# Column weights turned by VectorE and sread in eight array tiles, a fourth batch in seven products, and a new order, in a cross-attention and star-ReLU kernel

## The chip, the cores and the metric

The kernel runs on one core of a Trainium2 chip. The metric is device time in microseconds (us), the median of several runs. The engines are TensorE (PE; PEld is its weight load), VectorE (DVE), ScalarE (ACT), GpSimd (POOL) and SyncE (SP). Transfers are started from the queues of POOL (loads of x and of the weights), SP (first load of x, all stores) and ACT (small loads).

## The reference

```python
# x (8, 8, 512, 64), state (8, 8, 32, 64): batch, head, rows, D
scores = x @ state.T / 8;  a  = softmax(scores, over the 32 states);  xread = a @ state
scores2 = state @ x.T / 8; a2 = softmax(scores2, over the 512 rows);  sread = a2 @ x
t = concat([xread, sread], rows)           # per batch 544 tokens of 8 heads x 64 = 512
h = t @ w_in                               # (4352, 512) @ (512, 2048)
out = (s * relu(h)**2 + b) @ w_out         # (4352, 2048) @ (2048, 512)
```

All eight batches need both softmaxes of the same score matrix: over the states (for xread) and over the rows (for sread).

## The kernel before

The work of each batch `b` is cut into pieces. A list of words, `ORDER` (L15 to L75), names them in the order in which they are issued, and L713 calls them one after another, so that each engine's own order follows from the list. A word is a piece's name with its arguments: `M.5.3.0` is piece `M` for batch 5, weight block 3. A last letter A, V or G puts the piece on ACT, DVE or POOL. Eight heads are kept as two groups `g` of four; a group's four heads lie in the four quarters of the 128 partitions.

Scores and the first softmax. `x` (L177) loads a batch, cast to f16, from POOL's queue; for batches above 2 a tiny POOL copy (L180) first waits until the batch before it has been turned. Batch 0 comes as f32 over SP's queue (L211 to L216) and is cast by `castx`. `xT` (L283) turns it with DVE in 32x32 blocks of f32 pairs. `T` (L291) makes the scores: 16 products on 32x32 tiles of the array, all 512 rows moving. `keep` (L306) copies scores for later use. `U`, `mu`, `D`, `E1`, `z`, `At`, `A` are the softmax over the states on DVE and ACT, in turned form, with `A` the turned-back weights; `D` and `At` can stand on POOL.

Layer one of the x tokens. `M` (L423) multiplies the state with a block of `w_in` (tiles of 64 rows by 32 columns) and `Mc` (L437) copies the result from PSUM; `l` (L469, half-width `lh`) multiplies `A` by it, two products of 512 columns, followed by a relu on ACT (L456). `s` (`sh`) squares blocks of it. `L` (L492) is layer two in its plain form: four products of 512 columns per word, 16 words per batch, and `out` (L512) evicts and stores.

The second softmax. `nm`, `nms`, `E2`, `a2` form the weights over the rows. `aps` (L391) turns them with eight TensorE transposes per batch into PSUM, `a2T` (L397) copies them out, `xn` (L188) loads x again with its rows on partitions, and `V` (L400) makes sread: per batch 32 products with 128 rows and 64 columns of weights and 32 moving columns, in one of the two-bank PSUM buffers. A word may name two batches (`V.5.2`). `srd` (L420) copies the result into `srdT`. `lsr`, `ssr`, `S_sr`, `P_sr`, `ev_sr` are the two layers for the sread tokens of all batches together, at the end.

Seven products. For batches 5, 6 and 7, and for sread, layer two is done as a 2x2 block product in seven half-size products instead of eight: `wsum` (L522) forms sums of weight blocks, `S` (L555) sums of activation blocks (in two halves each), `P` (L575) is half a product, eight matmuls of 256 columns (14 words per batch), `ev` (L589) evicts a block into a running sum, seven per batch, and `put` (L597) stores.

PSUM: `two_banks` (L130) gives one of two buffers of two banks each, one for `own` pieces and one for the others; `T`, `M`, `aps`, `V` and a few others share them. Layer one has two banks, layer two and the seven products two.

Of the kernel before, what the change touches and what calls it, by code (L numbers as in the profile page):

```python
# [15 lines left out]
    "win.0 win.1 wout.0 x.1 win.2 wout.1 win.3 wout.2 wout.3 idle.11 castx.1.0.V castx.0.0.A xT.0.0.0 "  # L16
    "casts.A turn.0.4.A pair.0.4 xT.0.1.0 T.0.1.0 U.0.0 mu.0.0 sb castx.1.1.A castx.0.1.A D.0.V.0 "
    "xT.0.0.1 idle.6 xT.0.1.1 E1.0.0 T.0.0.1 keep.0.0 M.0.0.1 Mc.0.0.A z.0.0 At.0.V.0 A.0.0 idle.4 "
    "M.0.1.1 Mc.0.1.A lh.0.0.0 U.0.1 mu.0.1 D.0.V.1 lh.0.2.0 keep.0.1 sh.0.0.0.V sh.0.2.0.V E1.0.1 z.0.1 "
    "At.0.V.1 L.0.1.0 lh.0.6.0 sh.0.6.0.G L.0.0.0 M.1.0.1 Mc.1.0.A lh.0.4.0 A.0.1 lh.0.6.1 xT.1.0 "  # L20
    "sh.0.4.0.G xT.1.1 T.1.1 U.1 lh.0.0.1 lh.0.4.1 lh.0.2.1 sh.0.2.1.G mu.1 M.0.2.0 Mc.0.2.A L.0.0.1 x.2 "
    "L.0.1.1 st D.1.V sh.0.6.1.V keep.1 l.0.9 l.0.8 M.0.3.1 Mc.0.3.V l.0.10 s.0.8.2.V cps.0 cps.1 E1.1 "
    "l.0.13 z.1 l.0.11 s.0.10.2.V At.1.V M.1.1.1 l.0.12 Mc.1.1.A l.0.14 l.0.15 L.0.0.2 s.0.12.2.A M.1.2.1 "
    "A.1 s.0.14.2.V Mc.1.2.A cps.2 cps.3 c L.0.1.2 l.1.1",
    "l.1.0 sh.0.0.1.V xT.2 M.1.3.1 x.3 L.0.0.3 bias out.0.0 l.1.2 Mc.1.3.V l.1.3 L.0.1.3 out.0.1 L.0.2.0 "
    "pair.4.16 sh.0.4.1.G turn.4.12.A L.0.2.1 l.1.4 turn.12.16.V T.2.1 keep.2 s.1.0.4.V l.1.5 l.1.6 "
    "L.0.2.2 l.1.8 U.2 mu.2 l.1.7 L.0.2.3 out.0.2 D.2.V l.1.9 s.1.8.2.V l.1.15 M.2.1.0 E1.2 z.2 M.2.0.1 "
# [12 lines left out]
    "M.4.2.1 wsum.T4.0.V s.3.8.4.V M.4.1.0 L.2.3.0 L.2.2.3 out.2.2 l.3.13 l.3.15 L.2.3.1 l.3.14 xT.5 "  # L40
    "Mc.4.2.V s.3.14.2.V Mc.4.1.A s.3.12.2.V wsum.T4.1.V",
    "l.4.0 L.2.3.2 L.2.3.3 out.2.3 T.5.1 V.4 srd.4 nm.5 U.5 l.4.1 nms.5.A x.6 L.3.0.0 E2.5.0 L.3.0.1 nm.2 "
    "l.4.2 mu.5 E2.5.1 L.3.1.0 D.5.V l.4.3 s.4.0.4.V L.3.1.1 L.3.0.2 l.4.4 xn.5 l.4.5 E1.5 z.5 L.3.0.3 "
    "nms.2.A M.4.3.0 out.3.0 M.5.0.1 Mc.4.3.A L.3.1.2 l.4.7 xn.2 Mc.5.0.A a2.5 l.4.6 s.4.4.4.V At.5.V "
    "E2.2.1 L.3.1.3 l.4.8 E2.2.0 L.3.2.0 out.3.1 aps.5 a2.2 a2T.5.A xT.6 L.3.2.1 L.3.2.2 l.4.9 L.3.2.3 "
    "l.4.10 aps.2 a2T.2.V l.4.11 A.5 s.4.10.2.V L.3.3.0 l.4.13 M.5.2.1 Mc.5.2.A out.3.2 M.5.1.0 Mc.5.1.A",
    "l.5.0 L.3.3.1 L.3.3.2 l.4.14 l.4.12 L.3.3.3 s.4.12.2.V l.5.1 s.4.8.2.V l.4.15 L.4.0.0 out.3.3 "
    "s.4.14.2.V T.6.1 U.6 nm.6 V.5.2 srd.2 srd.5 l.5.3 nms.6.V nm.0 E2.6.1 l.5.2 E2.6.0 L.4.0.1 L.4.0.2 "
    "l.5.5 mu.6 D.6.V s.5.0.4.V L.4.0.3 out.4.0 E1.6 l.5.6 M.6.0.1 M.5.3.0 l.5.8 Mc.5.3.A x.7 xn.6 a2.6 "
    "L.4.1.0 L.4.1.1 L.4.1.2 z.6 l.5.4 nms.0.V L.4.2.0 Mc.6.0.A At.6.V l.5.7 s.5.4.4.V S.5.3.0.V E2.0.1 "  # L50
    "L.4.1.3 aps.6 L.4.2.1 L.4.2.2 E2.0.0 L.4.2.3 xn.0 out.4.1 a2T.6.A l.5.9 l.5.10 a2.0 aps.0 S.5.1.0.V "
    "L.4.3.0 L.4.3.1 l.5.11 xT.7 a2T.0.V s.5.8.4.V M.6.1.0 Mc.6.1.A A.6 M.6.2.1 out.4.2 l.5.13 l.5.12 "
    "s.5.12.2.V L.4.3.2 l.5.15 l.5.14 s.5.14.2.V L.4.3.3 P.5.0 out.4.3 Mc.6.2.A l.6.1 P.5.1 T.7.1 "
    "S.5.2.0.V S.5.3.1.V S.5.1.1.V V.6.0 srd.6 U.7 P.5.2 l.6.2 ev.5.X1 S.5.2.1.V",
    "l.6.0 keep.7 P.5.3 l.6.3 mu.7 S.5.4.0.V l.6.5 P.5.4 l.6.7 ev.5.Y srd.0 l.6.4 P.5.5 P.5.6 D.7.V E1.7 "
    "l.6.8 S.5.4.1.V P.5.7 l.6.6 M.6.3.0 s.6.0.4.V M.7.0.1 ev.5.X2 z.7 l.6.9 P.5.8 ev.5.W1 P.5.10 At.7.V "
    "Mc.7.0.A Mc.6.3.A s.6.4.2.V l.6.10 xn.7 P.5.9 s.6.6.2.V A.7 l.6.12 ev.5.X3 M.7.1.0 Mc.7.1.V M.7.2.1 "
    "nm.7 l.6.13 P.5.11 l.6.11 ev.5.W2 put.5.0.0 put.5.0.1 l.6.14 P.5.12 l.7.2 s.6.8.4.V S.6.3.0.V "
    "S.6.1.0.V P.5.13 Mc.7.2.A l.6.15 ev.5.X4",
    "l.7.0 s.6.14.2.V s.6.12.2.V S.6.3.1.V M.7.3.1 P.6.0 l.7.1 Mc.7.3.A l.7.6 P.6.1 put.5.1.0 nms.7.V "  # L60
    "E2.7.0 P.6.2 ev.6.X1 S.6.2.0.V S.6.1.1.V S.6.2.1.V put.5.1.1 l.7.12 l.7.3 E2.7.1 s.7.0.4.V P.6.3 "
    "a2.7 P.6.4 P.6.5 l.7.11 l.7.5 ev.6.Y aps.7 l.7.4 a2T.7.V S.6.4.0.V nm.1 nms.1.V P.6.6 l.7.8 ev.6.X2 "
    "l.7.15 V.7 srd.7 l.7.7 P.6.7 E2.1.1 E2.1.0 xn.1 P.6.8 P.6.9 ev.6.W1 a2.1 l.7.10 l.7.9 s.7.8.4.A "
    "S.6.4.1.V aps.1 s.7.4.4.V a2T.1.V ev.6.X3 P.6.10 P.6.11 ev.6.W2 put.6.0.0 put.6.0.1 l.7.14 "
    "s.7.14.2.V V.1 srd.1 S.7.3.0.V l.7.13 P.6.12 s.7.12.2.V P.6.13 P.7.0 lsr.6 S.7.1.0.V ev.6.X4 "
    "put.6.1.0 lsr.1 P.7.1 S.7.3.1.V S.7.2.0.V lsr.5 P.7.2 S.7.4.0.V P.7.3 lsr.2 lsr.3 ev.7.X1 P.7.4 "
    "ev.7.Y",
    "lsr.0 S.7.1.1.V S.7.2.1.V P.7.6 P.7.5 ssr.0.2.V lsr.9 ev.7.X2 ssr.2.2.V lsr.7 P.7.7 ev.7.W1 "
    "put.6.1.1 S.7.4.1.V lsr.8 ssr.8.2.V P.7.8 ssr.6.2.V lsr.4 ssr.4.2.V S_sr.3.0.V S_sr.1.0.V lsr.14 "
    "P.7.9 lsr.11 ev.7.X3 S_sr.2.0.V P.7.10 lsr.13 lsr.10 ssr.10.2.V P.7.11 ev.7.W2 lsr.12 S_sr.4.0.V "  # L70
    "lsr.15 put.7.0.0 ssr.14.2.V ssr.12.2.V S_sr.1.1.V P.7.12 put.7.0.1 P.7.13 S_sr.2.1.V P_sr.0 "
    "ev_sr.0.0.X.0.0 S_sr.3.1.V ev.7.X4 put.7.1.0 put.7.1.1 P_sr.1 S_sr.4.1.V P_sr.2 P_sr.3 "
    "ev_sr.0.1.X.0.0 P_sr.4 ev_sr.1.1.W.0.0 P_sr.5 ev_sr.1.1.X.1.1 ev_sr.0.0.Y.1.1 P_sr.6 ev_sr.0.1.W.1.1 "
    "ev_sr.1.0.X.0.1",
# [4 lines left out]
def kernel(  # L79
# [90 lines left out]
    srdT = konst.tile([P, NK, Ns, B], FP16, name="srdT")  # L170
# [5 lines left out]

    def load_x(b):  # L177

        if b > 2:
            nc.gpsimd.tensor_copy(ahead, at[b - 1]["xT"][0:1, 0, 0])  # L180
        xh_t[b] = xpool.tile([P, NG, NT, D], FP16, name=f"xh_{b}", tag="xh")
        for g in range(NG):
            nc.gpsimd.dma_start(
                out=xh_t[b][:, g].rearrange("p j d -> p (j d)"),
                in_=x[b, 4 * g : 4 * g + 4].rearrange("r (t j) d -> (r t) (j d)", j=NT),
            )

    def load_xn(b):  # L188

        xn_t[b] = xpool.tile([P, H, SCH, D], FP16, name=f"xn_{b}", tag="xn")  # L190
        for jh in range(4):
            nc.gpsimd.dma_start(  # L192
                out=xn_t[b][32 * jh : 32 * jh + 32].rearrange("t h c d -> t h (c d)"),
                in_=x[b].rearrange("h (t jh c) d -> jh t h (c d)", t=32, jh=4)[jh],
            )
# [15 lines left out]
    for p in range(2):  # L211
        for g in (1, 0):
            h = slice(NT // 2 * p, NT // 2 * p + NT // 2)
            nc.sync.dma_start(
                xf[g][:, h], x[0, 4 * g : 4 * g + 4].rearrange("r (t j) d -> (r t) j d", j=NT)[:, h]
            )  # L216
# [174 lines left out]
    def at_aps(b):  # L391
        at[b]["aps"] = aps = blocks(two_banks(f"aps_{b}", FP16), 0)
        for g in range(NG):
            for c in range(SCH):
                transp(aps[:, SCH * g + c], at[b]["a2"][:, g, P * c : P * c + P])
# [351 lines left out]
```

## Time and profile before

| what | value |
|---|---|
| median of 3 runs | 224.83 us (224.76 to 225.58) |
| the profiled execution | 224.36 us |
| its span in the profile | 222.2 us |
| granted TensorE clock | 1.00 |
| loads and stores | 22.67 MB in 23416 packets |

"Busy" is the time in which an engine has at least one instruction running. Ends of matmuls are modelled, and one matmul's record overlaps the next; their pace is read from the distance between starts. In the chain of waits, a piece lasts until the next piece begins. The groups of instructions give the mean length of one instruction, line by line:

```profile
L462 DVE TENSOR_TENSOR g<-r 128x2048 f16<-128x2048 f16 x16 | 19.4, 1214 | 2.2 <-ACT r L456 2.1
L462 DVE TENSOR_TENSOR g<-r 128x1024 f16<-128x1024 f16 x23 | 15.2, 677 | 6.0 <-ACT r L456 6.0
...
L343 DVE TENSOR_TENSOR At<-E,rz 128x1024 f16<-128x1024 f16 x7 | 9.1, 1294 | 0.0
...
L421 ACT CAST srdT<-vps 128x128 f16<-128x128 f32 x8 | 5.7, 774 | 5.3 <-PE vps L137 5.3
```

The fields are line, engine, operation, output and inputs by the program's names, shapes, count; then busy us and mean ns of one; then the engine's idle time just before them and what ended it.

### The profile page before, as it was taken

How to read it: one execution, taken by the hardware profiler on the slowest of the kernel's cores; microseconds unless marked ns; L12 is line 12 of the kernel's file. 1: busy time of each engine (PE TensorE's matmuls, PEld its weight loads, DVE VectorE, ACT ScalarE, POOL GpSimd, SP SyncE). 2: the span in 40 equal slices, each digit the busy share in tenths (PEclk: the TensorE clock that was granted, in tenths of full speed). 3: DMA queues.
4: the chain of work that ended last, by engine and by line, in shares of the span. 5: the costliest groups of instructions: out<-in, count | busy, mean ns of one | idle time of the engine just before them, and what ended most of it. 6: DMA issues, size and time to landing. Idle time of an engine off the chain costs nothing.

```text
span 222.2 us, 4473 instructions
## 1 busy us (share of the span) xinstructions
PE 210.7 (95%) x1816; PEld 115.8 (52%) x1816; DVE 183.6 (83%) x267; ACT 141.8 (64%) x243; POOL 43.4 (20%) x73
## 2 busy tenths in 40 slices
PE   6469999999999999999999999999999999999992
PEld 2234334444444443444454544457766778888881
DVE  1597998889769997989796799889999997966772
ACT  2475895776488869855787479485877858533400
POOL 8245504000273400046002160005200000000000
PEclk9999999999999999999999999999999999999999
DMA  6999993420557892048927397226903500440066
GB/s 158 227 207 206 205 193 58 101 72 20 100 112 117 112 174 50 16 100 120 192 47 133 96 128 124 49 45 101 141 2 65 127 0 3 94 99 0 3 134 149
DMA packets 23416, 22.67 MB, mean 102 GB/s; under 512 B 4196, under 2 KB 16996, under 8 KB 23396
## 3 DMA queue, kind: packets, MB, share of 16 engines
q0 software_dynamic: 16560, 12.26, 38.6%
q1 hardware_dynamic: 6160, 9.97, 18.2%
q8 instruction: 14, 0.23, 0.4%
q10 hardware_dynamic: 676, 0.16, 0.3%
q14 instruction: 6, 0.05, 0.1%
HBM read 25.72 MB, written 8.91 MB: 156 GB/s over the span
## 4 chain that ended last, share of the span: by engine, by line
PE 88%; DMA 4%; DVE 3%; ACT 3%; SPq 1%; issue 0%
PE ops L496 31%; PE hps L452 24%; PE opf_X L137 9%; PE opf_W L137 5%; PE mps L137 4%; DMA xf<-in_x_dram 4%; PE hps_sr L452 3%; PE opf_Y L137 2%; PE vps L137 2%; PE T_None L137 2%; PE aps L137 2%; PE ops_sr_X L137 2%; ACT M L152 1%; DVE xT L289 1%; PE ops_sr_W L137 1%; ACT rh L482 1%
## 5 line engine op out<-in xcount | busy, mean ns | idle before, releaser
L456 ACT ACTIVATE r<-hps 128x512 f16<-128x512 f32 x120 | 69.3, 610 | 29.8 <-PE hps L452 28.4
L496 PE MATMUL ops<-w_out,g 128*128 128x512 f16 x320 | 78.1, 379 | 1.3 <-DVE g L462 1.3
L452 PE MATMUL hps<-A,M 128*128 128x512 f16 x240 | 65.3, 380 | 0.5 <-DVE M L152 0.3
L496 PEld LDWEIGHTS <-g 128*128 128x128 f16 x320 | 30.3, 98 | 38.4 <-issue 2.8
L462 DVE TENSOR_TENSOR g<-r 128x1024 f16<-128x1024 f16 (+1 forms) x39 | 34.5, 897 | 8.1 <-ACT r L456 8.0
L452 PEld LDWEIGHTS <-M 128*128 128x128 f16 x240 | 21.9, 98 | 25.8 <-issue 4.7
L137 PEld LDWEIGHTS <-g 128*128 128x128 f16 x288 | 28.0, 98 | 6.4 <-issue 0.2
L152 ACT CAST M<-mps 128x1024 f16<-128x1024 f32 x28 | 28.0, 1013 | 1.8 <-PE mps L137 1.8
L192 POOL DMA_DIRECT2D xn<-in_x_dram x32 | 18.5, 588 | 29.2 <-PE vps L137 28.3
L506 DVE SCALAR_TENSOR_TENSOR osb<-ops,sb_bc,bias_bc 128x512 f32<-128x512 f32 x20 | 14.7, 734 | 1.0 <-PE ops L496 1.0
L180 POOL COPY ahead<-xT 1x2 f16<-1x2 f16 x5 | 1.8, 367 | 67.0 <-DVE xT L289 67.0
L456 ACT ACTIVATE r_sr<-hps_sr 128x256 f16<-128x256 f32 x16 | 6.2, 385 | 12.8 <-PE hps_sr L452 12.4
L564 DVE TENSOR_TENSOR g<-g 128x1024 f16<-128x1024 f16 x18 | 12.2, 685 | 2.0 <-PE opf_Y L137 1.9
L289 DVE STREAM_TRANSPOSE xT<-xh 128x1024 f32<-128x1024 f32 (+2 forms) x12 | 10.3, 871 | 3.2 <-ACT xh L152 3.2
L333 DVE TENSOR_REDUCE z<-E 128x32 f32<-128x1024 f16 (+1 forms) x9 | 9.9, 1095 | 3.7 <-ACT E L328 3.7
L137 PE MATMUL opf_X<-w_T,g 128*128 128x256 f16 x96 | 11.9, 273 | 0.0
L137 PE MATMUL mps<-w_in,stT 64*32 64x512 f16 x256 | 11.2, 383 | 0.2 <-ACT M L152 0.2
L318 DVE TENSOR_REDUCE mu<-U 128x32 f32<-128x1024 f32 (+1 forms) x9 | 9.9, 1097 | 0.2
L376 ACT ACTIVATE E<-T_None,nms 128x512 f16<-128x512 f32 x8 | 5.5, 691 | 6.9 <-DVE nms L372 4.4
L328 ACT ACTIVATE E<-Dm 128x1024 f16<-128x1024 f32 (+1 forms) x9 | 8.7, 963 | 1.8 <-DVE Dm L322 1.5
L322 DVE TENSOR_TENSOR Dm<-U,mu 128x1024 f32<-128x1024 f32 (+1 forms) x8 | 9.6, 1201 | 0.2
L314 DVE STREAM_TRANSPOSE U<-T_None 128x1024 f32<-128x1024 f32 x7 | 8.7, 1247 | 1.2 <-PE T_None L137 0.8
(94 smaller groups left out, 259.4 us busy)
## 6 DMA issues: line engine op xcount, KB each, us to landing
out_dram<-osb SPq DMA_DIRECT2D x32, 128.0 KB, 2.7
xn<-in_x_dram POOLq DMA_DIRECT2D x32, 128.0 KB, 5.7
xh<-in_x_dram POOLq DMA_DIRECT2D x14, 256.0 KB, 5.2
out_dram<-osx SPq DMA_DIRECT2D x24, 128.0 KB, 2.4
w_in<-in_moe_w_in_dram POOLq DMA_DIRECT2D x8, 256.0 KB, 10.6
w_out<-in_moe_w_out_dram POOLq DMA_DIRECT2D x4, 512.0 KB, 12.7
xf<-in_x_dram SPq DMA_DIRECT2D x4, 256.0 KB, 7.5
out_dram<-osb SPq DMA_DIRECT2D x4, 256.0 KB
```

The source lines that it names most:

```text
L137: return nc.tensor.matmul(out, lhsT, rhs, start=start, stop=stop, tile_position=tp, is_transpose=is_transpose, skip_group_check=skip,)
L152: (engine.copy if engine is nc.scalar else engine.tensor_copy)(out, in_)
L192: nc.gpsimd.dma_start(out=xn_t[b][32 * jh : 32 * jh + 32].rearrange("t h c d -> t h (c d)"), in_=x[b].rearrange("h (t jh c) d -> jh t h (c ...
L289: nc.vector.transpose(part(out, p, g), part(in_, p, g))
L318: nc.vector.tensor_reduce(part(mu, p), blk(part(at[b]["U"], p)), AX.X, ALU.max)
L333: nc.vector.tensor_reduce(part(z, p), blk(part(at[b]["E1"], p)), AX.X, ALU.add)
L452: nc.tensor.matmul(hps, lhsT, rhs, start=(i == 0), stop=(i == len(terms) - 1))
L456: nc.scalar.activation(R_t[tag, q][:, i], hps, AF.Relu)
L462: e.tensor_mul(g, r, r)
L496: nc.tensor.matmul(ops_t[tag, rr], G_t[tag][:, f, P * rr : P * rr + P], w_out_f(f), start=(f == 0), stop=(f == NKF - 1),)
L506: nc.vector.scalar_tensor_tensor(osb, ops_t.pop((tag, rr)), s_bc, bias_bc, ALU.mult, ALU.add)
L564: e.tensor_tensor(out, x, y, op)
```

## The change

1. `aps` and its copy are gone. `a2T` is one DVE turn in 32x32 blocks of f32 pairs, like `A`.
2. To fit that, a head's 512 rows are laid out otherwise: `xn` is loaded in 3 transfers with the rows of a head in a quarter of the partitions (before: 4 transfers, shorter runs); `x` is loaded in 4 transfers per batch instead of 2; `T` reads x in another order of columns (`in_order`); heads and partition quarters are paired by `hp ^ 2 * g` instead of `hp ^ g`; `out` and `put` write runs of one row instead of two.
3. `V` is 128 products per batch, each with 32 rows by 64 columns of weights, going round eight tiles of the array, into two two-bank buffers instead of one. `srd` is two copies of 64 columns.
4. Batch 4 takes the seven products too (`S.4`, `P.4`, `ev.4`, `put.4` for `L.4`, `out.4`). Block sums can be made in one piece for both halves (`HALVES`, third argument 2).
5. `ORDER` is new throughout. Among what it moves: `x.1` stands ahead of the weights on POOL's queue; there are 13 warming matmuls (`idle`) at the start instead of 21; 32 vector pieces stand on POOL instead of 5 (four `At`, two `D`, twelve `s`, six `S`, three `wsum`, three `sh`, two `S_sr`); more squares stand on ACT, more `Mc` on DVE.

```diff
-    def at_aps(b):
-        at[b]["aps"] = aps = blocks(two_banks(f"aps_{b}", FP16), 0)
-        for g in range(NG):
-            for c in range(SCH):
-                transp(aps[:, SCH * g + c], at[b]["a2"][:, g, P * c : P * c + P])
-
-    def at_a2T(b, e):
-        copy(e, sm(b, "a2T", [P, NG * SCH, P], FP16, apool, 2), at[b]["aps"])
+    def at_a2T(b):
+        a2T = sm(b, "a2T", [P, NG, NT // 2, Ns, 2], FP16, apool, 2)
+        nc.vector.transpose(
+            a2T.rearrange("p g v n e -> p (g v n e)").bitcast(FP32),
+            at[b]["a2"].rearrange("p g s -> p (g s)").bitcast(FP32),
+        )
...
-            for k in range(NK):
+    def at_V(b):
+        pair = at[b]["vps"] = [two_banks(f"vps_{b}_{i}", own=i) for i in range(2)]
+        a2T, xn = at[b]["a2T"], xn_t[b]
+        for j in range(NT):
+            e, v = j // (NT // 2), j % (NT // 2)
+            for hp in range(4):
                 for g in range(NG):
-                    hp = k ^ g
-                    for i in range(SCH):
+                    r, rows = hp ^ 2 * g, slice(32 * hp, 32 * hp + 32)
                         mm(
-                            vps[D * g : D * g + D, k, :],
-                            xn[:, 4 * g + k, i, :],
-                            a2T[:, SCH * g + i, Ns * hp : Ns * hp + Ns],
-                            start=(i == 0),
-                            stop=(i == SCH - 1),
-                            tp=(0, D * g),
+                        pair[r // 2][D * g : D * g + D, r % 2, :Ns],
+                        xn[rows, g, j, :],
+                        a2T[rows, g, v, :, e],
+                        start=(j == 0),
+                        stop=(j == NT - 1),
+                        tp=(32 * hp, D * g),
                         )
...
     def at_srd(b):
-        nc.scalar.copy(srdT[:, :, :, b], at[b]["vps"])
+        for i in range(2):
+            nc.scalar.copy(srdT[:, 2 * i : 2 * i + 2, b], at[b]["vps"][i][:, :, :Ns])
...
     def load_x(b):
...
-        for g in range(NG):
+        for g, u in np.ndindex(NG, 2):
             nc.gpsimd.dma_start(
-                out=xh_t[b][:, g].rearrange("p j d -> p (j d)"),
-                in_=x[b, 4 * g : 4 * g + 4].rearrange("r (t j) d -> (r t) (j d)", j=NT),
+                out=xh_t[b][:, g, NT // 2 * u : NT // 2 * u + NT // 2].rearrange("p v d -> p (v d)"),
+                in_=x_u(b, g, u).rearrange("r t v d -> r t (v d)"),
             )
...
     def load_xn(b):
-        xn_t[b] = xpool.tile([P, H, SCH, D], FP16, name=f"xn_{b}", tag="xn")
-        for jh in range(4):
+        xn_t[b] = xpool.tile([P, NG, NT, D], FP16, name=f"xn_{b}", tag="xn")
+        for g, k, n in ((0, 0, 4), (1, 0, 2), (1, 2, 2)):
+            h = 4 * g + (k ^ 2 * g)
             nc.gpsimd.dma_start(
-                out=xn_t[b][32 * jh : 32 * jh + 32].rearrange("t h c d -> t h (c d)"),
-                in_=x[b].rearrange("h (t jh c) d -> jh t h (c d)", t=32, jh=4)[jh],
+                out=xn_t[b][32 * k : 32 * k + 32 * n, g].rearrange("p j d -> p (j d)"),
+                in_=x[b, h : h + n].rearrange("r (t j) d -> (r t) (j d)", j=NT),
             )
...
+    HALVES = (slice(0, 4), slice(4, 8), slice(0, 8))
```

The start of the new order, as far as the prediction speaks of it (the first word on TensorE is `turn.0.4.A`):

```diff
-    "win.0 win.1 wout.0 x.1 win.2 wout.1 win.3 wout.2 wout.3 idle.11 castx.1.0.V castx.0.0.A xT.0.0.0 "
...
+    "castx.1.0.A x.1 xT.0.1.0 casts.V castx.0.0.V turn.0.4.A pair.0.4 xT.0.0.0 castx.1.1.A T.0.1.0 U.0.0 "
+    "mu.0.0 D.0.V.0 E1.0.0 z.0.0 xT.0.1.1 At.0.V.0 win.0 win.1 keep.0.0 idle.2 idle.8 win.2 castx.0.1.A "
+    "xT.0.0.1 M.0.0.1 Mc.0.0.A idle.3 T.0.0.1 keep.0.1 A.0.0 lh.0.0.0 M.0.1.1 Mc.0.1.A wout.0 M.1.0.0 "
+    "Mc.1.0.A U.0.1 mu.0.1 xT.1.0 lh.0.2.0 win.3 st D.0.V.1 E1.0.1 wout.1 sh.0.0.0.V M.1.2.1 Mc.1.2.A "
+    "lh.0.4.0 sh.0.4.0.G xT.1.1 lh.0.6.0 M.0.2.0 T.1.1 sh.0.2.0.V L.0.0.0 wout.2 z.0.1 Mc.0.2.A At.0.V.1 "
+    "A.0.1 lh.0.0.1 U.1 l.0.8 L.0.1.0 keep.1 mu.1 lh.0.2.1 l.0.11 M.0.3.0 Mc.0.3.V M.1.1.1 l.0.9 l.0.10 "
+    "D.1.G E1.1 l.0.15 pair.4.16 s.0.8.2.V x.2 lh.0.6.1 sh.0.6.0.V turn.4.12.A s.0.10.2.V L.0.0.1 l.0.14 "
+    "l.0.13 wout.3 z.1 At.1.V A.1 L.0.1.1 l.0.12 L.0.1.2 lh.0.4.1 L.0.0.2 l.1.2 sb M.1.3.1 l.1.9 "
+    "sh.0.6.1.G Mc.1.1.V l.1.11 Mc.1.3.A s.0.14.2.V cps.0 cps.1 cps.2 cps.3 l.1.3",
```

And the places behind `V` that the prediction names:

```diff
+    ... xn.3 out.1.1 x.5 a2T.3 V.3 z.3 srd.3 l.2.13 l.2.6 s.2.0.2.G s.2.2.2.G M.3.3.1 ...
+    ... l.5.7 P.4.2 V.2 D.6.G srd.2 out.3.2 l.5.0 l.5.8 ev.4.X1 S.4.1.0.V S.4.3.1.V S.4.1.1.V V.5 srd.5 l.5.3 xT.7 l.5.4 M.5.3.0 ...
```

## The prediction, made before the changed kernel was run

> **What bounds the kernel now.** I read the page's busy shares and chain first, then the table of stretches, then single stages in the timeline.
>
> ```profile
> PE 210.7 (95%) x1816; PEld 115.8 (52%) x1816; DVE 183.6 (83%) x267; ACT 141.8 (64%) x243; POOL 43.4 (20%) x73
> ...
> PE 88%; DMA 4%; DVE 3%; ACT 3%; SPq 1%; issue 0%
> ```
> ```profile
> 12.00:21.00 9.00, 7.27 (x80) 3.40 (x72) 8.18 (x15) 6.32 (x10) 3.66 (x6) 1.00 1.21 208
> 21.00:33.00 12.00, 11.26 (x104) 4.25 (x103) 10.76 (x12) 10.34 (x17) 4.09 (x5) 1.00 1.30 201
> 33.00:60.00 27.00, 27.00 (x185) 11.59 (x182) 23.47 (x31) 16.69 (x29) 3.60 (x7) 1.00 0.31 66
> 60.00:100.00 40.00, 40.00 (x298) 17.30 (x304) 35.07 (x47) 31.80 (x51) 11.01 (x17) 1.00 0.56 100
> ```
> The second view gives, per stretch, its length and the busy time of PE, PEld, DVE, ACT and POOL, then clock, DMA share and GB/s. From 33 us PE is never idle (27.00 of 27, 40.00 of 40; the later stretches to 212 us are the same). So TensorE work taken out of that part comes off the time one for one, while what DVE, ACT or POOL gain or lose counts only where PE is made to wait. Before 33 us it is latency: transfers (about 200 GB/s), then the first batch's softmax.
>
> The prices of TensorE work are in the chain of waits in order of time (start, length, what), where a length runs to the next piece, so that overlapped ends are not counted twice:
>
> ```profile
> 67.85 0.45 PE aps L137 x8
> ...
> 80.86 0.64 PE vps L137 x32
> ...
> 85.50 1.73 PE ops L496 x8
> ...
> 126.12 1.14 PE vps L137 x64
> ...
> 200.67 0.87 PE opf_X L137 x8
> ```
>
> **What is removed and added on TensorE.**
> - The eight `aps` (eight transposes each) go: 8 x 0.45 = 3.6 us off.
> - Layer two of batch 4: 64 products of 512 columns, 8 x 1.73 = 13.84 us, become 14 pieces of eight with 256 columns, 14 x 0.87 = 12.2 us: 1.6 us off.
> - `V`: 32 products per batch before, four bursts alone or behind `T` (0.64) and two of two batches (1.14), 4.84 us in all. After: 128 products of 32 rows by 64 columns, 32 moving columns each, eight bursts. What one such burst costs the trace does not show. The rows beside it:
>
> ```profile
> 80.79 0.70 PE L137 MATMUL vps<-a2T,xn 128*64 128x32 f16 x32
> ```
> ```profile
> 77.52 0.64 PE L137 MATMUL T_None<-xT,stE 32*32 32x512 f16 x16
> ```
> ```profile
> 77.52 0.14 PEld L137 LDWEIGHTS <-stE 32*32 32x32 f16 x16 [0.42 <-issue]
> ```
> The first is today's `V`: one product is recorded with 183 ns, so the starts are (0.70 - 0.18) / 31 = 16.7 ns apart, 0.53 us for 32. If products on the small tiles also follow each other at 16.7 ns, 128 take 2.14 us. The other two rows are `T`, eight 32x32 tiles in use: its 16 products of 512 columns take 0.64 us, where one after another at the 216 ns of the `ops` row they would need 3.5 us, so tiles in different rows and columns do run side by side. Its 16 weight loads (88 ns each) start (0.14 - 0.09) / 15 = 3.5 ns apart: at that pace 128 take 0.45 us. The new `V` goes round eight tiles, so each tile gets 16 products, as each column half does now. I take 0.53 us, today's value, because `T` is the nearest row in what matters here (tiles in turn); ends 0.45 and 2.14 are kept. So 8 x 0.64 = 5.12 us: 0.3 more. The bursts that leave the 128x128 shape number 33 before and 34 after (counted in the order), so changes of shape add nothing worth a term.
>
> Here a rule of the Trainium skill speaks against the change. TensorEngine Tiling (Array Packing), Instruction Overhead, gives each matmul about 60 cycles whatever its width and advises against taking a tiling factor from a dimension that is already small; TensorE: Matmul & The Clock Gate, Back-to-back issue gap, puts that at about 25 ns. By it 128 products would take an estimated 3.2 us and the kernel 241.7 us. The trace does not agree: `vps` already runs at 16.7 ns.
>
> **What moves to other engines.** DVE, by the rows of groups: `At` of four batches to POOL (4 x 1.29 off), two `D` to POOL and one back (1.4 off), squares 12 fewer of 2048 columns (1.21) and 8 fewer short ones (19 off in all), the sums that the seven products need (`S`) +0.5 net of those that go to POOL, evictions of batch 4 +2.3, eight turns of `a` at 0.71 (the row of `A`) for four copies at 0.67: +3.0, five more `Mc` at 1.21: +6.1, weight and sread sums 2.6 off. Together about -16: 168 of 220 us. ACT: four copies of `a2T` and five `Mc` off (9.2), 17 more squares at 0.6 to 1.9 (17 on); `srd` becomes two copies of 64 columns written in runs of 32; the 256-column relu takes 0.385, so I put 0.25 on each instead of one at 0.77. Together +6: 148. POOL: 32 vector pieces instead of 5 (1.06 per 512 f16 columns, 1.91 per 1024 f32): 63 us instead of 6; 14 more issues for x, 8 fewer for xn at about 0.58: 104 of 220. None reaches PE's share, and the cover is PE's own work ahead; cost 0, with what remains under waits.
>
> **Waits.** (1) POOL against DVE:
>
> ```profile
> 24.16 1.04 POOL L462 TENSOR_TENSOR g<-rh 128x512 f16<-128x512 f16 x1 [2.24 <-ACT rh L482]
> 24.17 2.11 DVE L322 TENSOR_TENSOR Dm<-U,mu 128x1024 f32<-128x1024 f32 x1
> ```
> `D` takes 1.25 elsewhere and 2.11 here, started 10 ns behind a POOL operation: it stood still for most of it. The turns and reductions beside other POOL operations keep their time. SBUF — State Buffer, Who interferes with whom, of the Trainium skill says the same: a DVE operation with two SBUF inputs and a GpSimd one exclude each other. After the change DVE has some 57 us of two-input operations and POOL is computing in about 30% of the time: of some 60 such operations 19 would meet one and wait about 1 us, half a POOL operation, 19 us in all; DVE would be at 187, 85%, about where it is now. (2) `V` now holds both two-bank buffers (L130), so the next `M` or `T` on PE waits for `srd` on ACT, and behind it every layer-one product. The order puts two layer-one products (0.86 us) behind `V.3`, `V.2` and `V.5`, against 0.1 + 2 x 0.25; at the old 0.77 each it would cost 0.8 us three times. (3) `D.1` on POOL stands ahead of the loads x.2 and wout.3; w_out's last quarter is needed at `cps.3`. By bytes at 205 GB/s it lands near 33 us (it has x.2 and st ahead of it now); PE has 3 us more work ahead of `cps.3` than before, when it stood at 32.5 us: covered. I charge 0.5 us for all three (ends 0 and 6).
>
> **The head.** x.1 now goes first on POOL's queue (four issues, 2.3 us) and w_in.0 behind it, 0.52 MB / 205 GB/s = 2.6 us later, near 12 us; w_out.0 is fifth instead of third, near 19.7 us. Before, `M.0.0` ran at 12.18 and the first layer two at 16.55 us. Against that `E1.0.0` no longer stands behind the last cast on ACT, and `M.1` and `T.1` fill PE meanwhile: 4.5 us of real work done by 19.7 us against 5.1 before. I take 0, ends -1.5 and +2. `T` reads x in runs of 32 columns: 0, because its rows already read every second element; at half pace +3. Stores in 2 KB instead of 4 KB runs: 0, DMA share is 0.3 to 0.7 there and four `osb` buffers cover it. The tail (seven products, one eviction, one store) is as before: 0.
>
> **Sum.** 224.36 (the profiled execution, span 222.2 and 2.16 around it) - 3.6 - 1.6 + 0.3 + 0.5 = 220.0. The median is 0.47 above that execution, so **220.4 us**.
>
> **Rivals.**
> - *V runs in file* (slower): weight loads or issue of the small tiles do not overlap, 128 x 16.7 = 2.14 us, +1.61 per batch, +12.8: **233.2**. It decides from the pace at which 4.4 us are eaten: 0.53 + 0.55 = 1.08 us per burst, 8.5 ns per product. For it: no row shows more than 16 pairs at 3.5 ns, and `V`'s 64 columns take longer to load than `T`'s 32. Against: `T`. 0.16.
> - *Only the two column halves overlap*: 64 x 16.7 = 1.07 us, +4.3: **224.7**, no change. 0.08.
> - *POOL's work comes late*: PE waits for a quarter of the 19 us: **225**. For it: the row of `D`, and the third stage of the order (layer one of batch 2), where POOL has 22 us of work in 22 us of PE's. Against: PE's lead, and DVE's 16 us. 0.14.
> - *More than forecast* (a better head, 0.45 per burst): **217.5** or less, 0.04.
> - Forecast, 217.5 to 222.5: 0.58.
>
> **Chances.** 0.5% (1.1 us) is about what a measurement can tell. Below 223.7: 0.58 + 0.04 + 0.04 of the two middle cases = 0.66. Within: 0.13, the rest of these two. Above 225.9: 0.16 + late POOL 0.05 = 0.21. The range leaves out the file and a little at the bottom: 216.5 to 228.
>
> **What would show it.** A `vps` burst of 128 products in 0.6 to 0.7 us (2.2 if in file); no `aps`; `opf` 56 pieces of 0.87; PE at 100% from 33 us on, with idle "<-POOL" only in fractions; POOL near 104 us; DVE two-input operations stretched beside POOL's; first layer two near 20 us. I am wrong if PE shows gaps of several us before `P.4`, or behind the weights in the first 35 us.

## The result, and the profile after

| | before | after |
|---|---|---|
| median | 224.8 us | 255.76 us (255.46 to 256.49, 4 runs) |
| ratio | 1 | 1.1375 (95% interval 1.1343 to 1.1407) |
| profiled execution, span | 224.36, 222.2 us | 255.46, 253.7 us |
| mean granted clock | 1.00 | 0.963 |

The change makes the kernel 14% slower; 220.4 us had been forecast, in a range to 228. From the page of the changed kernel:

```profile
span 253.7 us, 5988 instructions
...
PE 215.0 (85%) x2560; PEld 122.5 (48%) x2560; DVE 170.4 (67%) x239; ACT 147.5 (58%) x263; POOL 106.2 (42%) x106
...
PE 61%; DMA 20%; issue 5%; DVE 5%; POOL 4%; ACT 2%; SPq 1%; DVEq 0%; POOLq 0%
```

DVE, ACT and POOL came out as forecast (168, 148 and 104). TensorE's busy time grew by 4 us although 5.2 us of work went, and its share fell from 95 to 85%. In the chain, transfers went from 4 to 20% and "issue" from 0 to 5%: these two are the trail. The stretches, in the columns of before (length; busy PE, PEld, DVE, ACT, POOL; clock, DMA share, GB/s):

```profile
0.00:12.00 12.00, 0.39 (x2) 0.13 (x2) 1.23 (x4) 2.27 (x3) 5.58 (x12) 1.00 0.76 118
12.00:21.00 9.00, 4.37 (x26) 1.51 (x26) 3.07 (x6) 1.04 (x2) 1.39 (x2) 1.00 0.90 137
21.00:33.00 12.00, 8.05 (x75) 2.87 (x76) 7.38 (x14) 7.08 (x11) 3.77 (x5) 0.72 1.13 156
33.00:60.00 27.00, 24.18 (x177) 10.73 (x177) 20.41 (x25) 19.22 (x33) 14.54 (x16) 1.00 0.81 107
60.00:100.00 40.00, 38.63 (x383) 16.45 (x381) 28.67 (x34) 31.03 (x49) 23.34 (x23) 1.00 0.57 103
```

The first stretch of before, which the prediction does not show:

```profile
0.00:12.00 12.00, 7.05 (x53) 2.77 (x53) 5.13 (x12) 4.98 (x9) 6.92 (x15) 1.00 0.94 193
```

In the first 21 us TensorE did 4.8 us where it had done 14.3, and the transfers ran at 118 and 137 GB/s where they had run at 193 and 208. TensorE is no longer at 100% behind 33 us: its idle gaps over 250 ns from 30 us to its last product add up to 11.1 us, where before had none. Four places carry the loss.

*The head.* Batch 0's casts on ACT, each waiting for its quarter of x (start, length, what, then the idle time before it and its releaser). First the last cast of before, then two of the changed kernel:

```profile
10.36 0.62 ACT L152 CAST xh<-xf 128x512 f16<-128x512 f32 x1 [1.38 <-DMA xf<-in_x_dram]
```
```profile
19.96 0.62 ACT L152 CAST xh<-xf 128x512 f16<-128x512 f32 x1 [11.05 <-DMA xf<-in_x_dram]
23.00 0.62 ACT L152 CAST xh<-xf 128x512 f16<-128x512 f32 x1 [1.41 <-DMA xf<-in_x_dram]
```

x arrives 12.6 us later; the first layer two starts at 33.79 instead of 16.55 us.

*V.* The chain in order of time has one burst of `V` in two:

```profile
113.42 1.12 PE vps L137 x125
114.53 2.71 issue
117.24 0.20 PE vps L137 x3
```

TensorE stands for 2.71 us with nothing that the profile shows to wait for, three products short of the end. A second burst, at 150.45, stands for 1.06. Without such a stop a burst takes 1.145 us up to the next product, against 0.64 before.

*A store.* In the timeline, DVE's eviction `ev.6.X1` writes the one buffer `osx_0`, which batch 5's stores have not left yet, and TensorE waits behind it for 3.12 us:

```profile
203.20 0.75 DVE L608 SCALAR_TENSOR_TENSOR osx<-opf_X,sb_bc,bias_bc 128x512 f32<-128x512 f32 x1 [3.94 <-DMA out_dram<-osx]
```

*The tail.* The last eviction of before, and of the changed kernel:

```profile
218.18 0.48 DVE L695 SCALAR_TENSOR_TENSOR osr<-ops_sr_X,sb_bc,bias_bc 128x256 f32<-128x256 f32 x1 [0.39 <-PE ops_sr_X L137]
```
```profile
246.33 0.48 DVE L710 SCALAR_TENSOR_TENSOR osr<-ops_sr_X,sb_bc,bias_bc 128x256 f32<-128x256 f32 x1 [0.39 <-PE ops_sr_X L137]
```

Each ends 0.48 us later, and the span runs on: 222.2 - 218.66 = 3.5 us before, 253.7 - 246.81 = 6.9 after. This difference is easily missed, since no engine is busy in it.

Besides, the clock was granted at half for 6.8 us from 23 us on, behind the waits of the head, and for 3.4 us at 153 and at 204 us, behind V.5's stop and the store's; before had none of this.

### The profile page after: what moved, and what is told of

Same layout as the page of the kernel before. It is cut to its first block, busy times and chain, and to the rows that moved or that the text cites. A ratio compares the mean times of both kernels' runs of the same rounds, so it can differ in the third digit from the quotient of the medians.

```text
span 253.7 us, 5988 instructions
## 1 busy us (share of the span) xinstructions
PE 215.0 (85%) x2560; PEld 122.5 (48%) x2560; DVE 170.4 (67%) x239; ACT 147.5 (58%) x263; POOL 106.2 (42%) x106
## 3 DMA queue, kind: packets, MB, share of 16 engines
q1 hardware_dynamic: 6064, 9.97, 15.8%
## 4 chain that ended last, share of the span: by engine, by line
PE 61%; DMA 20%; issue 5%; DVE 5%; POOL 4%; ACT 2%; SPq 1%; DVEq 0%; POOLq 0%
PE hps L465 17%; PE ops L509 13%; PE opf_X L137 10%; DMA xh<-in_x_dram 8%; DMA w_in<-in_moe_w_in_dram 6%; PE opf_W L137 6%; PE vps L137 4%; DMA w_out<-in_moe_w_out_dram 4%; PE hps_sr L465 3%; PE mps L137 2%; PE opf_Y L137 2%; DMA out_dram<-osx 2%; POOL xh L187 2%; PE ops_sr_X L137 1%; PE T_None L137 1%
## 5 line engine op out<-in xcount | busy, mean ns | idle before, releaser
L509 PE MATMUL ops<-w_out,g 128*128 128x512 f16 x256 | 61.5, 379 | 0.0
L475 POOL TENSOR_TENSOR g<-r 128x1024 f16<-128x1024 f16 (+1 forms) x12 | 26.4, 2210 | 39.6 <-ACT r L469 39.6
L475 DVE TENSOR_TENSOR g<-r 128x1024 f16<-128x1024 f16 (+1 forms) x24 | 19.0, 804 | 4.8 <-ACT r L469 4.8
L187 POOL DMA_DIRECT2D xh<-in_x_dram x28 | 19.4, 698 | 0.9 <-POOLq L746 0.8
L473 ACT ACTIVATE g<-r 128x1024 f16<-128x1024 f16 (+1 forms) x14 | 17.9, 1298 | 0.2
L608 DVE SCALAR_TENSOR_TENSOR osx<-opf_X,sb_bc,bias_bc 128x512 f32<-128x512 f32 x12 | 9.0, 749 | 13.1 <-PE opf_X L137 7.6
L152 DVE CAST M<-mps 128x1024 f16<-128x1024 f32 x9 | 11.0, 1217 | 6.1 <-PE mps L137 5.6
L137 PE MATMUL vps<-a2T,xn 32*64 32x32 f16 x1024 | 10.4, 192 | 3.8 <-issue 3.8
L579 DVE TENSOR_TENSOR g<-g 128x1024 f16<-128x1024 f16 (+1 forms) x15 | 12.9, 858 | 0.3
L137 PEld LDWEIGHTS <-xn 32*64 32x64 f16 x1024 | 9.3, 102 | 6.9 <-issue 6.7
```

The costliest lines, as they stand in the source:

```text
L137: return nc.tensor.matmul(out, lhsT, rhs, start=start, stop=stop, tile_position=tp, is_transpose=is_transpose, skip_group_check=skip,)
L152: (engine.copy if engine is nc.scalar else engine.tensor_copy)(out, in_)
L187: nc.gpsimd.dma_start(out=xh_t[b][:, g, NT // 2 * u : NT // 2 * u + NT // 2].rearrange("p v d -> p (v d)"), in_=x_u(b, g, u).rearrange("r ...
L473: nc.scalar.activation(g, r, AF.Square)
L475: e.tensor_mul(g, r, r)
L509: nc.tensor.matmul(ops_t[tag, rr], G_t[tag][:, f, P * rr : P * rr + P], w_out_f(f), start=(f == 0), stop=(f == NKF - 1),)
```

## The experiments

Ratios are to the kernel before on the same chip, with 95% intervals. "x in runs" means that a transfer of x takes its 2 KB rows in a pattern that steps evenly through the 128 partitions; other rows of x then arrive than the reference needs.

### The head: whose pattern is it?

x_runs and x_xf_runs, the changed kernel with x in runs, in the later loads alone and in all:

```diff
-                in_=x_u(b, g, u).rearrange("r t v d -> r t (v d)"),
+                in_=x[b, 4*g : 4*g+4].rearrange("r (t w) d -> (r t) (w d)", t=32)[:, 512*u : 512*u+512],
... x_xf_runs as well, first load, as in before:
-                xf[g][:, h].rearrange("p v d -> p (v d)"), x_u(0, g, p).rearrange("r t v d -> r t (v d)")
+                xf[g][:, h], x[0, 4*g : 4*g+4].rearrange("r (t j) d -> (r t) j d", j=NT)[:, h]
```

> The changed kernel, in which each of the four transfers of a batch of x takes rows whose partition pattern is one even step (head and row merge), with the same count, sizes and 2 KB source runs; other rows of x arrive in a partition, so the output is another one. Theory A (the split partition pattern, four heads by 32 rows, makes each row of a transfer carry three 4-byte packets and holds up the queue and the first load of x beside it): about 14 us less, 242 us, first layer two near 19 us, 4-byte packets on the software queue near 1000 instead of 11792. Rival B (x.1 ahead of the weights is what delays the start): no change, 255.8 within 1. Rival C (the first load of x on SP's queue is slow by its own new pattern): no change.

> As x_runs, and the first load of x on SP's queue in the old form too. Theory A: as x_runs within 1 us (242). Rival C: 14 us less than x_runs, 242 where x_runs is at 256. If both patterns matter, each gives part.

Measured: x_runs 249.49 (1.111, 1.1009 to 1.121), x_xf_runs 234.37 (1.0397, 1.0331 to 1.0463). before_split turns it round: the kernel before, with only its later loads in the changed pattern.

> The kernel before, with only x loaded by four transfers of the split pattern, in its old place in the queue (after w_in.0, w_in.1 and wout.0); other rows arrive in a partition, so the output is another one. Theory A: x.1 and everything behind it on the queue are late, 5 to 10 us more, 230 to 235. Rival B (the place in the queue): no change, 224.8 within 1.5.

Measured: 226.86 (1.0077, 1.0044 to 1.0109). So the later loads cost 2 us by themselves and 6 in the changed kernel (x_runs), where the head stayed as it was, and the first load 15. Theory A missed twice: the later loads were to be worth 14 us in x_runs and 5 to 10 in before_split. before_xf_split puts the first load alone to the test:

```diff
-                xf[g][:, h], x[0, 4 * g : 4 * g + 4].rearrange("r (t j) d -> (r t) j d", j=NT)[:, h]
+                xf[g][:, h].rearrange("p v d -> p (v d)"),
+                x[0, 4*g : 4*g+4].rearrange("r (u t v) d -> u r t v d", u=2, t=32)[p].rearrange("r t v d -> r t (v d)"),
```

> The kernel before, with one edit: the first load of x on SP takes the rows in the changed kernel's split pattern (four heads by 32 runs on the partitions, 2 KB each); all the later loads of x, its products and its order stay, so only the rows of batch 0 differ. Theory C (the pattern of the first load alone costs the head its time: few packets of it are in flight, 6 or 7 where the old form had 17): the last of its packets ends near 22 us where before had 9.4, the first layer two starts 10 us or more later than before's 16.55 us, and the run is 10 to 14 us over before, 235 to 239 us. Theory A (the pattern is slow only beside the software queue's four-byte packets, of which this kernel has as few as before): last packet within 12 us, run within 3 us of before. If the pattern is slow but the products after it can wait, 228 to 233.

Measured: 242.64 (1.0806, 1.0773 to 1.0839), 18 us lost by one access pattern, over the range of 10 to 14. The first layer two starts 18.0 us later than in before (34.55), since x's last packet ends at 26.9 us where 22 had been expected. Its casts:

```profile
22.17 0.62 ACT L152 CAST xh<-xf 128x512 f16<-128x512 f32 x1 [4.68 <-DMA xf<-in_x_dram]
27.42 0.62 ACT L152 CAST xh<-xf 128x512 f16<-128x512 f32 x1 [4.64 <-DMA xf<-in_x_dram]
```

The trace's packet records say why. The first load is 512 packets of 2 KB in every one of these kernels, and each takes about 0.1 us; what differs is how many are under way at once:

| kernel | pattern of the first load | in flight, median (most) | last packet ends |
|---|---|---|---|
| before | 128 even steps | 10 (19) | 9.4 us |
| after | 4 heads of 32 | 4 (7) | 22.0 us |
| x_runs | 4 heads of 32 | 3 (6) | 26.2 us |
| x_xf_runs | 128 even steps | 11 (18) | 8.3 us |
| before_xf_split | 4 heads of 32 | 3 (5) | 26.9 us |
| x_heads | 32 rows, 16 transfers | 6 (14) | 15.8 us |

In the changed pattern the DRAM side of a transfer begins with a step over four heads, which does not merge with the 32 rows of a head. The Trainium skill, DMA: Bandwidth & Descriptors, Rules for kernel authors ("Use all 16 engines"), says that the slowest dimension of the two sides sets how many of the 16 transfer engines a transfer uses, and that an outermost one of fewer than 16 entries, here four, confines it to at most that many. The packets agree (at most 7 in flight against 19). So do the small packets of 4 bytes beside them: each transfer of the first load has 16 of these in before, x_xf_runs and x_heads, and 4 in the kernels with the four-head pattern. Which engine took a packet the trace does not tell.

x_heads looks for a remedy that keeps the rows: one transfer per head, 32 partitions each, and x.1 behind win.1.

```diff
+            for r in range(4):
+                nc.sync.dma_start(
+                    xf[g][32*r : 32*r+32, h].rearrange("p v d -> p (v d)"),
+                    x[0, 4*g + r].rearrange("(u t v) d -> u t (v d)", u=2, t=32)[p],
+                )
... and load_x likewise, 8 transfers of 32 partitions for each batch
```

> The changed kernel with x and the first x loaded head by head, 32 partitions a transfer (eight transfers per batch on POOL's queue, sixteen on SP's for the first), to the same places as in the changed kernel, and x.1 behind w_in.0 and w_in.1. Theory (the four-head pattern is what holds up the head): near x_xf_runs, 234 to 238, the first loads in by 11 us. If the small number of engines per transfer comes from the count of partitions rather than from the four-head pattern: as slow as the changed kernel, 250 or more.

Measured: 240.83 (1.0673, 1.0599 to 1.0746), over the 234 to 238 expected. It wins back 15 of the 21 us, part of which x.1's new place may have given; a transfer over 32 partitions is not slow by itself. The 16 issues on SP alone take 11.2 us.

### V: what its products cost

v_half leaves out every second product of `V` in the changed kernel (`for j in range(0, NT, 2)`); runs_vhalf does so in x_xf_runs; v_n64 lets each product move 64 columns instead of 32, also in x_xf_runs.

> The changed kernel with every second of the products of V left out: 64 per batch instead of 128. If the pace of 8 ns per product between starts and the supply of instructions price V: 8 x 64 x 8 ns = 4.1 us less for the pace, and the two long waits inside V (2.9 and 1.2 us) gone or shorter: 248 to 252. If V were bound by its eight entries and exits into the tile shape alone: no change.

> As x_xf_runs, with V's products over 64 moving columns instead of 32 (both halves of the turned pairs; twice the arithmetic, the result is another one). Theory: what prices a product of V is the supply of instructions, 8 ns for a load and a product, not the stream: a burst of 128 stays at 1.02 us from first to last start and the kernel at 234.4 within 1. Rival, the tiles run one after another or share a limit that goes with columns: a burst grows to 1.5 to 2 us, the kernel by 4 to 8 us.

> x_xf_runs with every second product of V left out (64 of 128 a batch; half of the sum of V is missing, so the rows differ). Theory (V pays 8 ns a product and instruction supply stands behind it): bursts of 0.61 us to the next instead of 1.145, 8 of them, so 4.3 us; the 1.3 us stand inside V.5 gone, and with it the slow window at 131 us, 1.7 us; in all 5.5 to 7.5 us, 227 to 229 us. Rival (the bursts lie beside other waits, and V's time comes back as waits on its evictions or on VectorE): 231 to 234 us.

Measured: v_half 245.01 (1.0882, 1.0782 to 1.0982), 10.8 us less and below the 248 to 252 expected; runs_vhalf 227.19 (1.0122, 1.0099 to 1.0146), v_n64 234.42 (1.0413, 1.0327 to 1.0499) beside x_xf_runs' 234.37. In runs_vhalf half the products take 0.612 us to the next product instead of 1.145, with no stop inside; twice the columns take 1.172, 0.03 us more. So a product costs 8 ns with 32 columns or 64, and 64 products fewer per batch are worth 7.2 us, of which the pace explains 8 x 0.533 = 4.3. The stop in V.5 (1.3 us between two starts) is gone too; that the remaining 1.6 us is the half clock behind it fits the length of that window (3.4 us), but was not tried by itself.

The pace is not even. The first 32 products of a burst start within 0.14 us, 4.5 ns apart; then comes a gap of 86 ns, and from the 33rd on they start 8.3 ns apart.

### The other waits

v_apart moves V.5 behind P.4.4 in x_xf_runs; osx2 gives `osx_0` two buffers there (and the other output tiles three instead of four); all_mended does both.

```diff
-    tile(..., name=f"osx_{b}_{key}", tag=f"osx{key}", bufs=1)
+    tile(..., name=f"osx_{b}_{key}", tag=f"osx{key}", bufs=2 if key == "0" else 1)
```

> As x_xf_runs, with V of batch 5 moved behind P.4.4, so that it does not follow V of batch 2 after two layer-one products. Theory (two bursts of 256 instructions each outrun the instruction transfer, and PE stands 1.3 us and then has half the clock for 3.4 us): the wait inside V and the slow window go, 2.5 to 3 us less, near 231.5. Rival (the wait belongs to V's operands): it moves with V, 234.4.

> x_xf_runs with osx_0 in two buffers (and the other output tiles in three instead of four, for the space). Theory: the 3.2 us in which TensorE stands before opf_X of batch 7's products, behind the eviction that waits for batch 5's stores, is a wait that this sets, and the slow window at 183 us follows from it. Then wait and window are gone and the run is 3.2 plus up to 1.7 us under x_xf_runs, 229.5 to 231 us. Rival: the eviction finds another thing late (S3, the adds on VectorE) and the run stays within 1 us of x_xf_runs, 233.5 to 234.5. If three output tiles are too few, new waits stand before the L groups of layer two and the run is over 234.5.

> x_xf_runs with osx_0 in two buffers and V.5 moved behind P.4.4 (as osx2 and v_apart together). If the three costs are separate: 234.4 less 3.2 for the stores, less 1.7 for the slow window after them, less 0.5 to 1.5 for V.5, 228 to 229.5 us. What is then left over before's 224.8 is V itself (8 bursts at 0.51 us more than before, 4.1 us). Rival: with one wait gone another of the order by hand is next, and the run stays over 231 us.

Measured: v_apart 233.83 (1.0386, 1.0288 to 1.0485), osx2 233.44 (1.0408, 1.0356 to 1.046), all_mended 232.70 (1.0349, 1.0315 to 1.0382). None of the three is told apart from x_xf_runs by its interval, and all three theories missed (231.5, 229.5 to 231, 228 to 229.5); all_mended's rival, over 231, holds. In v_apart the stop in V.5 and the slow window behind it did go, so the stop did not belong to V's operands. In osx2 the store wait of 3.1 us is gone, but V.1, which had run through, now stops for 2.0:

```profile
191.05 1.02 PE L137 MATMUL vps<-a2T,xn 32*64 32x32 f16 x105
194.07 0.28 PE L137 MATMUL vps<-a2T,xn 32*64 32x32 f16 x23 [2.00 <-issue]
```

The time is that of osx2's rival, but not for its reason, since no eviction waits there any more: a later stop took the place of the wait. I read it so: a string of short products uses up instructions faster than they are brought, any stop of TensorE lets the supply catch up, and where there is none, V itself stops. Two runs on all_mended try this: mended_vhalf leaves out half of V's products, v_split does each `V` as 64 and 64 with one or two layer-one groups or a product of layer two between (`V.1.0 l.7.14 V.1.1`).

> all_mended with every second product of V left out (half of V's sum is missing and x in runs, so the rows differ). all_mended had no store wait but stood 1.64 us inside V.1 and had a slow window behind it. Theory (V costs by its number of products, and the wait inside V.1 is of the same kind): bursts 0.53 us shorter, 8 times, 4.2 us; the wait of 1.6 us and the window, up to 1.7 us, gone: 225 to 226.5 us from 232.7. Rival (the store wait's end was repaid elsewhere for good, V has little to do with it): 228.5 to 231 us.

> all_mended with each V in two parts of 64 products, one or two layer-one groups or a product of layer two between them; all 1024 products are there (x in runs, so rows differ). Theory (instructions run out in a long string of short products, and a pause refills them): no wait inside V, so 1.6 us and its slow window of up to 1.7 us gone; pace as before, 2 x 0.61 us a batch against 1.145, 0.6 us more: 229.5 to 231.5 us. Rival (the wait comes at a fixed number of instructions, whatever stands between): the wait moves to another part of V or behind it, 232.5 to 234 us.

Measured: mended_vhalf 223.98 (0.9956, 0.9923 to 0.9989), v_split 230.74 (1.024, 1.0169 to 1.0311) against all_mended's 232.70. v_split lies in its theory's range, though its interval only just ends below all_mended's: the stop in V.1, 1.65 us between two starts, became 0.31, and V.0's 0.19 went, with all 1024 products in place. Half the products take 8.7 us off, more than the 6.2 to 7.7 expected.

That the supply of instructions is what stops V is supported by the packet records. In these kernels nine bursts stop for 1.0 us or more, and each goes on 1.36 to 1.57 us after the end of a 16 KB instruction transfer. The stops also keep their place: after the 42nd product of V.5 in all six kernels in which V.5 follows V.2 so closely with 128 products, and after the 105th of V.1 in osx2 and all_mended, where v_split has its 0.31 too. But a burst can lie beside such a transfer without a stop (V.7 in the changed kernel), and the supply was not measured by itself.

### The tail

mended_vhalf_tail is mended_vhalf with sread's columns and rows in the order of before:

```diff
-    out_sr = out_BSn[:, S:ST, :].rearrange("(r b) t n -> r b t n", r=2)
+    out_sr = out_BSn[:, S:ST, :].rearrange("b (r t) n -> r t b n", r=2)
... srdT likewise [P, NK, Ns, B]
```

> mended_vhalf with the part of sread's result in the order of before (srdT as n, b; the last stores' rows as 16 tokens by 8 batches instead of 4 batches by 32 tokens); still half of V's products left out and x in runs, so the rows differ. Theory (a transfer whose outermost step has four entries keeps 6 or 7 packets in flight, one of 16 keeps 17 to 20; it is the same cause at the head and at the tail): from the last eviction to the end of the span 3.5 us as in before instead of 6.9, and the run 3.4 us shorter than mended_vhalf's 224.0, 220.0 to 221.5 us, where the prediction had 220.4 for the whole change. Rival (the stores of batch 6 and 7 in the same queue make the tail long, whatever the pattern): tail 6 to 7 us, 223.5 to 224.5 us.

Measured: 220.71 us (0.9807, 0.9781 to 0.9833). Its last eviction, span 218.5:

```profile
214.58 0.48 DVE L710 SCALAR_TENSOR_TENSOR osr<-ops_sr_X,sb_bc,bias_bc 128x256 f32<-128x256 f32 x1 [0.39 <-PE ops_sr_X L137]
```

It starts at almost the same time as in mended_vhalf (214.64), and what follows its end takes 3.5 us instead of 6.9. Each of the last four stores has 19 to 21 packets in flight at most and takes 0.7 us, much as in before (18 to 20); with four batches outermost it was 6 or 7, and 1.4 to 2.3 us. This is the head's cause, at the other end.

### The seven products and the order alone

before_seven gives the kernel before batch 4's seven products, placed by hand; before_seven_early moves four sums and an eviction ahead on DVE (`S.4.1.0.V S.4.2.0.V S.4.3.1.V S.4.1.1.V S.4.2.1.V l.5.5 P.4.3 ev.4.Y mu.6 D.6.V`).

> The kernel before with only batch 4 in seven products, written into its old order by hand. The sum of the prediction: 1.6 us less on TensorE, so 223.2, if DVE hides eight sums and three more evictions (7.8 us more in a stage of 32 us in which it has 28.5). If it does not: 2 to 4 us more, 226 to 229.

> before_seven with the sums S.4.1 and S.4.2 and the eviction ev.4.Y moved on VectorE ahead of mu.6, D.6 and s.5.0.4, where TensorE had stood 5.1 us for them and the clock was at half for 6.8 us behind it. Theory (the seven products are worth 1.6 us where their sums are in time): the wait and the slow window gone, 232.5 less 5.1 less up to 3.4: 223 to 225 us, and 223.2 if nothing else is late. Rival (what VectorE does for the seven products, eight sums of 0.65 us and four more evictions, is late at another place instead): 226 to 231 us, a new wait of 2 us or more before T.6, M.6 or A.6.

Measured: 232.51 (1.0337, 1.028 to 1.0393), over both sums (223.2, or 226 to 229), and 230.35 (1.0257, 1.0221 to 1.0293). TensorE's idle time, first in the one, then in the other:

```profile
138.81 1.46 PE L137 MATMUL opf_X<-w_T,g 128*128 128x256 f16 x6 [5.13 <-DVE g L564]
```
```profile
139.42 1.01 PE L452 MATMUL hps<-A,M 128*128 128x512 f16 x2 [2.69 <-ACT r L456]
```

The first wait fell to 1.0 us, and a new one on ACT's relu took its place; the rival holds. In before's order, with DVE at 83% and its sums and evictions added to it, the products save nothing in either place that I tried.

aps_form and aps_form_osx2 take the changed order with x, `aps` and `V` in the form of before (aps words put in by hand), and the second also two `osx_0`.

> The changed order and batch 4's seven products, but x, xn, the turned column weights (by TensorE, L391 of before, aps) and V in the form of before: 32 products a batch, rows as in the reference. Theory (the seven products and the order are worth what was forecast, the losses come from x's loads and from V): before's 224.7 less 1.6 for the products, and 3.3 plus up to 1.7 for the wait for batch 5's stores: 226 to 228.5 us, no wait inside V. Rival (the order itself is worse than before's): over 230 us.

> aps_form with osx_0 in two buffers and three other output tiles. Theory: without the wait for the stores 222.5 to 225 us, at or below before's 224.7. Rival (the wait's end is repaid by another one behind it, as in osx2): 226 to 228 us. If the order by hand, made for the other V, keeps aps or a2T late: over 228 us.

Measured: 239.41 (1.0643, 1.0557 to 1.0729) and 237.32 (1.0495, 1.042 to 1.057); the fastest executions took 236.0 and 235.8. Both theories missed. No store wait and no stop in V, but new waits where I put `aps` (waiting of TensorE in all, times, longest), here of aps_form:

```profile
PE mps L137 <- ACT a2T L152: 5.5, 2, 2.9
PE aps L137 <- DVE M L152: 2.2, 1, 2.2
```

My placing of `aps` costs some 8 us, so these two say nothing about the order's worth, except that it was made for its `V`.

## Why the prediction was wrong

With each cause undone in turn, times as ratios times 224.83:

| kernel | ratio | us | step |
|---|---|---|---|
| after | 1.1375 | 255.7 | |
| x_xf_runs: x's patterns | 1.0397 | 233.8 | -22.0 |
| all_mended: store buffer, V.5 | 1.0349 | 232.7 | -1.1 |
| mended_vhalf: half of V's products | 0.9956 | 223.8 | -8.8 |
| mended_vhalf_tail: last stores | 0.9807 | 220.5 | -3.4 |

The end is the forecast of 220.4, in a kernel that leaves out half of `V`'s products, whose `V` thus costs 0.61 us a batch (0.64 had been put), and whose transfers are spread. So what the prediction summed holds together as a sum; what it put at zero or priced by the wrong row made 35 us. The agreement to 0.1 us is luck: x_xf_runs and all_mended differ by less than their intervals.

- **"The head. I take 0, ends -1.5 and +2": wrong by some 20 us, the largest error.** The step counted x.1's issues and bytes at 205 GB/s and took it that a load of the same bytes takes the same time. It did not look at the first load at all, though the diff changes its pattern; before_xf_split shows 18 us for that edit. The bound that failed was the rate: x came at 1 MB in 19.6 us (2.4 to 22.0), 53 GB/s, where before needed 7.6 us.
- **"I take 0.53 us, today's value" for V: wrong by a factor of two, with stops on top.** It measured 1.02 us from first to last start and 1.145 to the next product, 8 x 1.145 = 9.2 us where before had 4.84: 4.3 more, where +0.3 was put. The rows of `T` that I used were 16 products long, and the first 32 of a burst do start quickly; from the 33rd on it is 8.3 ns, which no row of 16 can show. At 8.0 ns a product over the whole burst it is just under the breakeven of 8.5 that the first rival named, and close to the second rival's 1.07, but for another reason: the moving columns do not matter (v_n64), the number of products does. That a long burst can stop for 1 to 3 us was in no rival. In all, 8.8 us go with half the products.
- **"The tail (seven products, one eviction, one store) is as before: 0": wrong, 3.4 us** (mended_vhalf_tail). Counted were products, evictions and stores, which are the same; the new row order of sread's stores was not looked at.
- **"Stores in 2 KB instead of 4 KB runs: 0": the rate was not the matter, but a wait was missed.** The new order puts `ev.6.X1` so soon behind `ev.5.W2` (195.10 us in the timeline) that batch 5's stores from `osx_0`, 5.35 us in the chain from 197.73 on, are still under way; it stood 3.94 us. The packets are of 2 KB before and after, and a store's 64 start within 0.6 to 0.7 us in both where nothing else runs. Three of the four stores did so, by 199.2 us; the fourth's packets ran from 200.9 to 202.7, while the 256 packets of xn.1 (198.9 to 204.1) were under way. No working of mine followed the one buffer through the new order. By itself the wait was worth at most 1 us (osx2), since V.1 stopped in its place.
- **"I charge 0.5 us for all three" waits: size of the parts.** `cps` did stand 2.2 us for w_out's last quarter, which had been called covered; with x spread, it went (x_xf_runs), so it was a consequence of the head. The list of TensorE's waits in after has none on POOL of 0.3 us or more (mended_vhalf_tail has one of 0.9), so the third rival, POOL's work coming late, did not decide. Nor has it one on `srd`. The 19 us that VectorE was to stand beside POOL were some 2.6: 30 of its two-input operations overlapped one of POOL, and four were stretched by more than 30%.
- **-3.6 for `aps` and -1.6 for the products: the sum holds, the parts were not shown apart.** TensorE is busy for 204.9 us in mended_vhalf_tail against 210.7, of which 1.4 us are the eight fewer warming matmuls. In before's own order the products lose (before_seven, before_seven_early).
- **DVE 168, ACT 148, POOL 104: right** (170.4, 147.5, 106.2). DVE's 187, with its standing beside POOL added, was too much. A `srd` copy took 0.215 us where 0.25 was put.
- **Half clock: not in the working.** Three slow windows before the tail, 13.6 us at half rate, came behind the head's waits and two of the stops; mended_vhalf_tail has none.

No kernel here with all of `V`'s new products beats the one before: v_split, the nearest, is 2.4% behind and still has x in runs, and x_heads, which keeps the reference's rows, is 6.7% behind.

## What to carry to other kernels

When a diff changes the access pattern of a transfer, price it by the outermost step that does not merge, not by its bytes: a step of four left 4 of 10 packets in flight at the head (18 us) and 5 of 15 in the last stores (3.4 us). Price a string of small products by its number of instructions, and take a burst of 128 as unknown when the trace shows 16, since here the first 32 were quicker than the rest; then look for the stops that another wait hides today. Where the forecast says that an engine stays busy to the end, look too at what runs behind the last instruction.

## What the runs showed of the hardware

- 32x64 products in eight tiles, in a burst without a stop: the first 32 start 4.5 ns apart, then comes a gap of 86 ns (100 with 64 columns moving), and from the 33rd on they start 8.3 ns apart; over 128 this makes 8.0. In v_apart V.7 began in a slow window (182.89 to 186.30 us), and its products from the 33rd to the 72nd started 8.5 ns apart at half clock: this pace does not go with the granted clock. Before, 32 products of 128x64 started 16.8 ns apart. The Trainium skill, TensorE: Matmul & The Clock Gate, section "Wait — 56ns, not 53.3ns?", says that start to start never drops below about 25 ns, however few the columns. Here it does, and the measurement decides.
- Bursts of 128 stopped for 1.0 to 2.7 us in some places and not in others; bursts of 64 with work between stopped for 0.4 us at most.
- The transfers with the four-way step on POOL's queue brought 11,792 packets of 4 bytes there, against 944 before and 1,040 in x_runs: three more for each of the 3584 runs of 512 elements that these transfers load. Alone they cost little (before_split, 226.86 us against 224.98).
- Some stops of TensorE were followed by half clock (V.5's of 1.06 us and the store's of 3.1 in after), others not (V.4's of 2.71 us). Before the tail all such windows last 3.41 us or two or three times that (10.24 in before_xf_split), and those of one run start on one grid: 23.40, 153.10, 204.31 and 248.68 us in after are 38, 15 and 13 times 3.413 us apart. The Trainium skill, TensorE: Matmul & The Clock Gate, Part 1, gives a free-running window of about 3.4 us for the clock gate; lengths and grid agree. On this grid V.4's stop stands 1.0 us in one window and 1.7 in the next, V.5's 1.06 us in a single one, so the time stood in a window does not by itself tell which stop is followed by half clock; that stays open.
